# Attention in an interleaved transformer: a wait between two half products moved from VectorE to TensorE, two of four exponentials joined, and a new order of the operations of a key tile

## The chip, the cores and the metric

The kernel runs on one core of one Trainium2 chip. The metric is the device time of one execution in microseconds. Before the change three runs gave a median of 3538.99 us (3538.1 to 3539.18).

## The reference

Two layers are computed, each an attention block and a squared-ReLU block, on 2048 rows of 640 numbers, with 32 heads of 20 numbers. In short:

```python
def A(x, wqkv, wo):                       # 32 heads, Dh = 20
    q, k, v = split_heads(x @ wqkv)
    scores = einsum("bhqd,bhkd->bhqk", q, k) * Dh ** -0.5
    o = einsum("bhqk,bhkd->bhqd", softmax(scores), v)
    return merge_heads(o) @ wo

def B(x, w1, b1, w2, b2):
    h = maximum(x @ w1 + b1, 0)
    return (h * h) @ w2 + b2

for _ in range(2):
    x = x + A(layernorm(x))
    x = x + B(layernorm(x))
```

## The kernel before, in words

The work of a layer comes in stages: the products that give q, k and v; attention; the output product; the squared-ReLU block. The change touches attention alone.

**Blocks and tiles.** Heads are taken four at a time (8 groups) and queries 512 at a time (4 blocks of queries), so a layer has 32 blocks (`NBLK`). A block passes over the 2048 keys in 16 key tiles of 128 keys. The four heads of a group are h = 2p + par: `par` says in which half of TensorE's rows the head's q and k stand (rows 0 to 63 or 64 to 127), and `p` which of two tiles of numbers there. Two matmuls with different `par` use different rows of the array and can run at once.

**What one key tile needs.** Four score products (`score`, 128 keys x 512 queries, one for each head), each followed by an exponential on ScalarE from PSUM to SBUF; then the product with v (`pv`: four heads in four column groups of the array, eight matmul records in the profile since these run in full fp32). The row of ones beside v gives the sum of the exponentials.

**The maxima.** The softmax subtracts a maximum over the keys for each query. It is found two blocks ahead: further products of queries and keys (`by_queries`, the queries now in the partitions), which VectorE reduces to their maxima. Most are done a pair at a time: `smax` makes one 128 x 512 product and one reduction for each `par`. When a layer is in its steady part, 12 such pairs fall on 8 key tiles: 8 pairs as whole products (operations "m" for par 0 and "n" for par 1), and 4 pairs in halves. An operation "u" makes a 128 x 256 product of par 0 in the left half of a PSUM bank, an operation "w" the matching one of par 1 in the right half of the same bank, and one reduction takes both (`smax_half`). Since matmuls on two halves of the array's rows must not write to one bank at once, "w" waits for "u". Before the change this wait went through VectorE: a `nop` in VectorE's queue waits for the matmul of "u", and the matmul of "w" waits for that `nop`.

**What sets the order.** The order of issue is written out by hand as a string in `ORDERS`, one letter an operation: "a" and "b" are the next score products of par 0 and par 1, "m", "n", "u", "w" are those above, "V" is the product with v, which is one key tile behind the scores. In the steady part one string, that for 12 pairs, is repeated for 992 of the 1024 key tiles of the two layers (the last block of each layer uses `both_heads`, which has exponentials of two banks at once already). Each engine works its own queue in the order of issue; an instruction that waits holds those behind it.

**PSUM.** Eight banks: before the change the scores go round banks 0 to 3 (`ps_st`), so a score product waits for the exponential four before it. The products for the maxima use banks 4 to 6 (`turn`), and bank 7 holds the sum of "V". At the end of a block ScalarE copies bank 7 to SBUF (`finish`), and the first "V" of the next block waits for that copy.

In the profile of before, line 481 is `by_queries`, 596 the score product, 603 its exponential, 608 the product with v, 493 and 521 the reductions of whole products and of halves, 517 the `nop`, 621 the copy of bank 7, 1158 and 1165 the wide version in the last block of a layer.

Of the kernel before, what the change touches and what calls it, by code (L numbers as in the profile page):

```python
# [10 lines left out]
AF = mybir.ActivationFunctionType  # L11
# [21 lines left out]
SCALE = DH ** -0.5  # L33
# [6 lines left out]
def tile_layers(  # L40
# [11 lines left out]
    nc = tc.nc  # L52
# [42 lines left out]

    ps_st = Ring(0, 1, 2, 3)
    ps_pj = Ring(4, 5, 6, 7)
# [398 lines left out]

    halved = {}

    def two_columns(t):
# [11 lines left out]
    def smax_half(bank, t, p, sub, c, half, par, earlier=None):  # L511
# [9 lines left out]
        nc.vector.tensor_reduce(  # L521
            maxima(t)[:, p : p + 3 : 2, sub, c if not half else column(t, p, sub)],
            bank.rearrange("q (r k) -> q r k", r=2),
            axis=AX.X,
            op=ALU.max,
        )

    def step_one(t, p, sub, x, par):
# [55 lines left out]

    free = []

    def score(t, kt, h, es):

        p, par = divmod(h, 2)
        if p not in es:  # L590
            es[p] = weights[len(e_n) % len(weights)]
            e_n.append(t)
        dst = banks[:, free.pop(0), :] if free else ps_st("st")
        b = 64 * par
# [7 lines left out]
        )  # L602
        nc.scalar.activation(es[p][:, par, :], dst, AF.Exp, scale=SCALE)  # L603

    def pv(acc, t, kt, es, heads=(3, 2, 1, 0)):
        for h in heads:
            p, par = divmod(h, 2)
            nc.tensor.matmul(  # L608
                acc[32 * h : 32 * h + 32, :],
                v_t[t // NQB, kt // 8][:, kt % 8, 32 * h : 32 * h + 32],  # L610
                es[p][:, par, :],
                start=(kt == 0),
                stop=(kt == NKT - 1),
            )
# [100 lines left out]
    def qkv(first, x_src, rest, scores):  # L715
# [277 lines left out]
        13: "baanmbVmbanambbnbmVanbmnaVnaabnmbVanbmaanVnmbbanaVmnbmabVabbmmnaVm",  # L993
        12: "mbubanawV" * 8,
    }

    def attention(first, x_src, first_rows):
# [146 lines left out]
        def both_heads(p):  # L1144
# [6 lines left out]
            es = es_of.setdefault(i, {})  # L1151
            es[p] = weights[len(e_n) % len(weights)]
            e_n.append(t)
            state["bank"] = (state["bank"] + 2) % 6
            dst = banks[:, state["bank"] : state["bank"] + 2, :]
            for par in range(2):
# [7 lines left out]
                )  # L1164
            nc.scalar.activation(es[p], dst, AF.Exp, scale=SCALE)  # L1165
            if p:
# [13 lines left out]

        free.extend((5, 6))
        for o in "abab":
# [377 lines left out]
```

## Time and profile before

| | |
|---|---|
| median of three runs | 3538.99 us |
| the profiled execution's own time | 3538.19 us |
| its span in the trace | 3536.2 us |
| granted TensorE clock | 1.00 in every stretch |
| busy: TensorE matmul, VectorE, ScalarE, GpSimd | 3521.2, 2731.2, 2652.9, 809.5 us |
| the two steady stretches of attention (first to last 128 x 512 exponential) | 309.9 to 1340.4 us, 2066.2 to 3097.4 us |
| in the stretch 500 to 1000 us: TensorE, VectorE, ScalarE busy | 500.0, 460.1, 498.5 of 500 us |

Times in the trace are microseconds from the start of the span. TensorE's matmuls are pipelined, so their records overlap and its busy share says little; the starts of its matmuls tell its pace. A record of an instruction on ScalarE or VectorE may begin before the one ahead of it has ended, so their pace is read from the ends.

### The profile page before, as it was taken

How to read it: one execution, taken by the hardware profiler on the slowest of the kernel's cores; microseconds unless marked ns; L12 is line 12 of the kernel's file. 1: busy time of each engine (PE TensorE's matmuls, PEld its weight loads, DVE VectorE, ACT ScalarE, POOL GpSimd, SP SyncE). 2: the span in 40 equal slices, each digit the busy share in tenths (PEclk: the TensorE clock that was granted, in tenths of full speed). 3: DMA queues.
4: the chain of work that ended last, by engine and by line, in shares of the span. 5: the costliest groups of instructions: out<-in, count | busy, mean ns of one | idle time of the engine just before them, and what ended most of it. 6: DMA issues, size and time to landing. Idle time of an engine off the chain costs nothing.

```text
span 3536.2 us, 70757 instructions
## 1 busy us (share of the span) xinstructions
PE 3521.2 (100%) x26542; PEld 2264.2 (64%) x26542; DVE 2731.2 (77%) x5023; ACT 2652.9 (75%) x5208; POOL 809.5 (23%) x927
## 2 busy tenths in 40 slices
PE   9999999999999999999999999999999999999999
PEld 7897444444444446999988964444444444479998
DVE  8878999999999993456567789999999999824443
ACT  3778999999999995122237789999999999932221
POOL 6531444221221111111153201221211211211110
PEclk9999999999999999999999999999999999999999
DMA  9776555323211136734477652232232111376231
GB/s 304 274 233 175 172 156 157 109 70 82 57 48 49 46 110 209 249 106 111 135 269 249 197 150 76 65 82 61 67 82 59 46 48 43 115 226 238 75 82 38
DMA packets 377413, 452.78 MB, mean 128 GB/s; under 512 B 176642, under 2 KB 223746, under 8 KB 377070
## 3 DMA queue, kind: packets, MB, share of 16 engines
q1 hardware_dynamic: 376254, 445.89, 41.6%
q8 instruction: 209, 3.42, 0.4%
q10 hardware_dynamic: 816, 2.36, 0.2%
q14 instruction: 134, 1.10, 0.1%
HBM read 273.83 MB, written 174.30 MB: 127 GB/s over the span
## 4 chain that ended last, share of the span: by engine, by line
PE 95%; DVE 2%; ACT 1%; DMA 1%; issue 1%; POOL 0%; SPq 0%; DVEq 0%; ACTq 0%
PE banks L608 29%; PE banks L481 22%; PE banks L293 13%; PE banks L596 11%; PE banks L1326 10%; PE banks L331 9%; DVE mx L493 1%; ACT e L603 1%; PE banks L1158 0%; DMA q<-d_qk 0%; ACT e L1165 0%; DVE bst L244 0%; DVE xnT L257 0%; DVE x L252 0%; DMA d_qk<-ev 0%
## 5 line engine op out<-in xcount | busy, mean ns | idle before, releaser
L603 ACT ACTIVATE e<-banks 128x512 f32<-128x512 f32 x3968 | 2034.7, 613 | 10.3 <-PE banks L596 2.2
L493 DVE TENSOR_REDUCE mx<-banks 128x1 f32<-128x512 f32 x2094 | 1346.5, 686 | 187.2 <-PE banks L596 126.6
L481 PE MATMUL banks<-k,q 60*128 60x512 f32 x4568 | 1347.7, 374 | 3.0 <-DVE v L377 1.7
L481 PEld LDWEIGHTS banks<-k,q 60*128 60x128 f32 x4568 | 763.8, 184 | 848.5 <-DVE mx L493 824.8
L596 PE MATMUL banks<-q,k 62*128 62x512 f32 x3968 | 1132.1, 432 | 0.4 <-DVE mx L541 0.4
L608 PE MATMUL banks<-e,vg 128*32 128x512 f32 x8192 | 1091.0, 605 | 1.5 <-ACT e L1165 1.5
L596 PEld LDWEIGHTS banks<-q,k 62*128 62x128 f32 x3968 | 654.5, 184 | 99.8 <-ACT e L603 36.6
L521 DVE TENSOR_REDUCE mx<-banks 128x2 f32<-128x512 f32 x982 | 670.5, 683 | 0.0
L541 DVE CUSTOM_DVE_ANT_0 rl<-banks,rl 128x512 f32<-128x512 f32 x510 | 332.8, 689 | 101.1 <-PE banks L481 91.0
L1311 ACT ACTIVATE r<-banks,b_t 128x512 f32<-128x512 f32 x96 | 66.2, 689 | 420.1 <-PE banks L293 396.3
L331 PE MATMUL banks<-xnT,wqk 64*128 64x512 f32 x2400 | 378.8, 394 | 0.3 <-ACT mark_t L333 0.3
L533 ACT ACTIVATE rl<-banks 128x512 f32<-128x512 f32 x510 | 270.8, 597 | 98.2 <-PE banks L481 89.3
L1326 PE MATMUL banks<-w,h 128*128 128x320 f32 x2304 | 340.4, 309 | 0.0
L1326 PEld LDWEIGHTS banks<-w,h 128*128 128x128 f32 x2304 | 339.2, 188 | 1.2
L293 PE MATMUL banks<-xnT,w 128*128 128x512 f32 x1440 | 329.4, 389 | 0.0
L331 PEld LDWEIGHTS banks<-xnT,wqk 64*128 64x128 f32 x2400 | 286.1, 185 | 34.2 <-issue 2.4
L293 PEld LDWEIGHTS banks<-xnT,w 128*128 128x128 f32 x1440 | 269.6, 188 | 55.3
L608 PEld LDWEIGHTS banks<-e,vg 128*32 128x32 f32 x8192 | 161.1, 108 | 165.5 <-issue 78.4
L652 POOL TENSOR_TENSOR few<-few,minus_t 128x16 f32<-128x16 f32 x62 | 179.8, 2900 | 357.9 <-DMA few<-d_s 352.5
L271 POOL CAST mr<-nt 128x32 fp32r<-128x32 f32 x64 | 13.4, 209 | 963.7 <-DVE nt L567 963.7
L331 PE MATMUL banks<-wv,xnT 64*128 64x320 f32 x1920 | 199.4, 307 | 0.9 <-ACT mark_t L333 0.9
L331 PEld LDWEIGHTS banks<-wv,xnT 64*128 64x128 f32 x1920 | 187.3, 185 | 2.5 <-ACT mark_t L333 1.4
(89 smaller groups left out, 2094.2 us busy)
## 6 DMA issues: line engine op xcount, KB each, us to landing
q<-d_qk SPq DMA_DIRECT2D x242, 240.0 KB
d_qk<-ev SPq DMA_DIRECT2D x80, 512.0 KB
k<-d_qk SPq DMA_DIRECT2D x152, 240.0 KB
x<-d_x SPq DMA_DIRECT2D x84, 320.0 KB
d_qk<-ev SPq DMA_DIRECT2D x80, 256.0 KB
d_o<-ot SPq DMA_DIRECT2D x248, 80.0 KB
ot<-d_o SPq DMA_DIRECT2D x38, 512.0 KB
d_v<-v SPq DMA_DIRECT2D x32, 512.0 KB
```

The lines of the kernel that those rows point to most:

```text
L293: nc.tensor.matmul(dst, a, b, start=(n == 0), stop=(n == last))
L331: m = nc.tensor.matmul(ch["dst"][:, :width], *pair, start=first, stop=last)
L481: return nc.tensor.matmul(dst, q_t[t][b : b + 60, p, sub * P : (sub + 1) * P], k_t[t // NQB, c][b : b + 60, p, keys], start=True, stop=True,)
L493: nc.vector.tensor_reduce(maxima(t)[:, 2 * par + p, sub, c : c + 1], dst, axis=AX.X, op=ALU.max)
L521: nc.vector.tensor_reduce(maxima(t)[:, p : p + 3 : 2, sub, c if not half else column(t, p, sub)], bank.rearrange("q (r k) -> q r k", r=2), ...
L533: nc.scalar.activation(res, dst, AF.Relu)
L541: nc.vector.tensor_tensor_reduce(out=r, in0=dst, in1=r, scale=1.0, scalar=LEAST, op0=ALU.add, op1=ALU.max, accum_out=maxima(t)[:, 2 * par ...
L596: nc.tensor.matmul(dst, k_t[t // NQB, kt // 4][b : b + 62, p, (kt % 4) * P : (kt % 4 + 1) * P], q_t[t][b : b + 62, p, :], start=True, stop ...
L603: nc.scalar.activation(es[p][:, par, :], dst, AF.Exp, scale=SCALE)
L608: nc.tensor.matmul(acc[32 * h : 32 * h + 32, :], v_t[t // NQB, kt // 8][:, kt % 8, 32 * h : 32 * h + 32], es[p][:, par, :], start=(kt == 0 ...
L652: nc.gpsimd.tensor_tensor(few, few, minus_t, op=ALU.pow)
L1326: nc.tensor.matmul(dst[:, :HALF], hs[f][:, hx, i * P : (i + 1) * P], w_2.piece(at_2(f0 + f, hw, hf)), start=(f == 0 and (hx, hw) == THREE[0]),
```

## The change

Three things change, all in attention.

- The wait of "w" for "u". The matmul of "u" now adds one to a semaphore of its own, `first_half`, and the matmul of "w" waits on TensorE itself for its count. The `nop` on VectorE is gone.
- The exponentials. Each score product now has a bank of its own (`SPOT`): head 1 bank 0, head 3 bank 1, head 0 bank 2, head 2 bank 3. Heads 1 and 2 keep an exponential of 128 x 512 each; heads 3 and 0, which are issued second and third and stand in the neighbouring banks 1 and 2, get one of 128 x 1024. The number of banks for scores, four, is the same. The buffers of exponentials are paired in another way (`es`), with the same number of them.
- The order of a key tile goes from "mbubanawV" to "bumbawnaV".

```diff
-    ps_st = Ring(0, 1, 2, 3)
...
+    first_half = tc.alloc_semaphore("first_half")
+    firsts_done = [0]
...
         if earlier is None:
-            mark = nc.vector.nop()
-            after(mark, m)
-            return mark
-        after(m, earlier, "matmuls on two halves of the rows write to one bank in turn")
-        nc.vector.tensor_reduce(
+            firsts_done[0] += 1
+            m.then_inc(first_half, 1)
+            tc.no_tile_sem_insts.add(m.ins.name)
+            tc.add_to_no_dep_group(f"first half {firsts_done[0]}", m.ins)
+            return m, firsts_done[0]
+        m_1, n = earlier
+        m.wait_op(first_half, n, "sem-ge")
+        tc.declare_no_dep(m.ins, m_1.ins, reason="waits for the semaphore of the first half")
+        tc.declare_fence(m.ins, group=f"first half {n}")
+        r = nc.vector.tensor_reduce(
...
+    SPOT = {(0, 1): 0, (1, 1): 1, (0, 0): 2, (1, 0): 3}
 
     def score(t, kt, h, es):
 
         p, par = divmod(h, 2)
-        if p not in es:
-            es[p] = weights[len(e_n) % len(weights)]
+        pair = "two" if p == par else "one"
+        if pair not in es:
+            es[pair] = weights[len(e_n) % len(weights)]
             e_n.append(t)
-        dst = banks[:, free.pop(0), :] if free else ps_st("st")
+        alone = bool(free) or pair == "one"
+        es[h] = es[pair][:, 1 - par if p == par else p, :]
+        dst = banks[:, free.pop(0) if free else SPOT[p, par], :]
...
-        nc.scalar.activation(es[p][:, par, :], dst, AF.Exp, scale=SCALE)
+        if alone:
+            nc.scalar.activation(es[h], dst, AF.Exp, scale=SCALE)
+        elif 3 - h in es:
+            nc.scalar.activation(es[pair], banks[:, 1:3, :], AF.Exp, scale=SCALE)
...
-        12: "mbubanawV" * 8,
+        12: "bumbawnaV" * 8,
...
-        free.extend((5, 6))
+        free.extend((5, 6, 0, 1))
```

How the rows move is seen in one key tile of TensorE's queue. In these rows 128x512 at line 481 (480 after the change) is "m" or "n", 128x256 is "u" or "w", line 596 (607) is a score product, line 608 (621) the product with v, of which four make one "V". In brackets is what an instruction waits for, by the name of the counter: `Activation_49` counts ScalarE's instructions, `DVE_49` VectorE's, `DVE_sequencer_49` the `nop`. TensorE before:

```order
L481 MATMUL banks<-k_4785,q_9896 128x512 [waits DVE_49]
L596 MATMUL banks<-q_9390,k_5479 128x512 [waits Activation_49]
L481 MATMUL banks<-k_4785,q_9896 128x256 [waits DVE_49]
L596 MATMUL banks<-q_9390,k_5479 128x512 [waits Activation_49] x2
L481 MATMUL banks<-k_4785,q_9896 128x512 [waits DVE_49]
L596 MATMUL banks<-q_9390,k_5479 128x512 [waits Activation_49]
L481 MATMUL banks<-k_4785,q_9896 128x256 [waits DVE_sequencer_49]
L608 MATMUL banks<-e_4746,vg_9233 32x512 x2
L608 MATMUL banks<-e_4745,vg_9233 32x512 x2
```

and now:

```order
L607 MATMUL banks<-q_8345,k_5236 128x512 [waits Activation_49]
L480 MATMUL banks<-k_4472,q_8595 128x256 [waits DVE_49]
L480 MATMUL banks<-k_4472,q_8595 128x512 [waits DVE_49]
L607 MATMUL banks<-q_8345,k_5236 128x512 [waits Activation_49]
L607 MATMUL banks<-q_8345,k_5236 128x512
L480 MATMUL banks<-k_4472,q_8595 128x256 [waits first_half]
L480 MATMUL banks<-k_4472,q_8595 128x512 [waits DVE_49]
L607 MATMUL banks<-q_8345,k_5236 128x512 [waits Activation_49]
L621 MATMUL banks<-e_4746,vg_8698 32x512
L621 MATMUL banks<-e_4745,vg_8698 32x512 x2
L621 MATMUL banks<-e_4746,vg_8698 32x512
```

The half product "u" now comes second in the tile, straight behind the "V" of the tile ahead and one score product. "w" stands three places behind it, as before four, and is no longer the last ahead of "V". The third score product has no wait of its own any more, since the second's covers both banks.

On ScalarE two key tiles before are eight exponentials, here with the copy of bank 7 ahead of them:

```order
L621 COPY o_8658<-banks 128x512 [waits DMAHW6_49,DMAHW1_49,DMAHW7_49,DMAHW0_49,PE_49]
L603 ACTIVATE e_4747<-banks 128x512 [waits PE_49]
L603 ACTIVATE e_4748<-banks 128x512 [waits PE_49]
L603 ACTIVATE e_4747<-banks 128x512 [waits PE_49]
L603 ACTIVATE e_4748<-banks 128x512 [waits PE_49]
L603 ACTIVATE e_4743<-banks 128x512 [waits PE_49]
```

and now six:

```order
L634 COPY o_9333<-banks 128x512 [waits DMAHW5_49,PE_49,Pool_49]
L615 ACTIVATE e_4747<-banks 128x512 [waits PE_49]
L617 ACTIVATE e_4748<-banks 128x1024 [waits PE_49,Activation_49]
L615 ACTIVATE e_4747<-banks 128x512 [waits PE_49]
L615 ACTIVATE e_4743<-banks 128x512 [waits PE_49]
L617 ACTIVATE e_4744<-banks 128x1024 [waits PE_49,Activation_49]
L615 ACTIVATE e_4743<-banks 128x512 [waits PE_49]
```

One instruction a key tile is gone. The wide one waits for TensorE and for an exponential of ScalarE's own: that is the wide one of three key tiles earlier, which wrote to the same buffer.

More of the change, by code (lines that the diff above doesn't have):

```diff
@@ L526, in smax_half @@
         )
+        tc.declare_no_dep(r.ins, m_1.ins, reason="waits for the second half, which waits for the first")
     def step_one(t, p, sub, x, par):
@@ L602, in score @@
         )
-        nc.scalar.activation(es[p][:, par, :], dst, AF.Exp, scale=SCALE)
+        if alone:
+            nc.scalar.activation(es[h], dst, AF.Exp, scale=SCALE)
+        elif 3 - h in es:
+            nc.scalar.activation(es[pair], banks[:, 1:3, :], AF.Exp, scale=SCALE)
     def pv(acc, t, kt, es, heads=(3, 2, 1, 0)):
         for h in heads:
-            p, par = divmod(h, 2)
             nc.tensor.matmul(
@@ L610, in pv @@
                 v_t[t // NQB, kt // 8][:, kt % 8, 32 * h : 32 * h + 32],
-                es[p][:, par, :],
+                es[h],
                 start=(kt == 0),
@@ L1151, in both_heads @@
             es = es_of.setdefault(i, {})
-            es[p] = weights[len(e_n) % len(weights)]
+            e = weights[len(e_n) % len(weights)]
             e_n.append(t)
+            es[2 * p], es[2 * p + 1] = e[:, 0, :], e[:, 1, :]
             state["bank"] = (state["bank"] + 2) % 6
@@ L1164, in both_heads @@
                 )
-            nc.scalar.activation(es[p], dst, AF.Exp, scale=SCALE)
+            nc.scalar.activation(e, dst, AF.Exp, scale=SCALE)
             if p:
```

## The prediction

> **What bounds the kernel now.** I read the page first (span, busy times, chain), then the groups of instructions by line in the middle of attention, then the timeline of one key tile engine by engine, and last the starts of "V" over a block's end.
>
> ```profile
> span 3536.2 us, 70757 instructions
> PE 3521.2 (100%) x26542; PEld 2264.2 (64%) x26542; DVE 2731.2 (77%) x5023; ACT 2652.9 (75%) x5208; POOL 809.5 (23%) x927
> PE 95%; DVE 2%; ACT 1%; DMA 1%; issue 1%; POOL 0%; SPq 0%; DVEq 0%; ACTq 0%
> L603 ACT ACTIVATE e<-banks 128x512 f32<-128x512 f32 x3968 | 2034.7, 613 | 10.3 <-PE banks L596 2.2
> L493 DVE TENSOR_REDUCE mx<-banks 128x1 f32<-128x512 f32 x2094 | 1346.5, 686 | 187.2 <-PE banks L596 126.6
> ```
>
> The page alone would mislead. It gives TensorE 100% and 95% of the chain, yet by its group row ScalarE sits idle for only 10.3 us ahead of 3968 exponentials. Four of those make a key tile, so the changed string covers 992 tiles. The lines of one layer tell their pace (count, shortest, median and longest duration, first and last start):
>
> ```profile
> L603 ACT ACTIVATE e<-banks x1984: 589/603/732, 309.9 to 1340.4; 128x512 f32<-128x512 f32 x199
> ```
>
> 1030.5 us for 496 tiles is 2.077 us a tile. Which engine sets that? First TensorE, one tile (start, length):
>
> ```profile
> 801.80 0.49 PE L481 MATMUL banks<-k,q 60*128 60x512 f32 x1
> 801.80 0.49 PE L596 MATMUL banks<-q,k 62*128 62x512 f32 x1
> 802.13 0.28 PE L481 MATMUL banks<-k,q 60*128 60x256 f32 x1
> 802.13 0.51 PE L596 MATMUL banks<-q,k 62*128 62x512 f32 x2
> 802.37 0.39 PE L481 MATMUL banks<-k,q 60*128 60x512 f32 x1
> 802.48 0.43 PE L596 MATMUL banks<-q,k 62*128 62x512 f32 x1
> 802.60 0.31 PE L481 MATMUL banks<-k,q 60*128 60x256 f32 x1
> 802.85 1.06 PE L608 MATMUL banks<-e,vg 128*32 128x512 f32 x8
> 803.84 0.49 PE L481 MATMUL banks<-k,q 60*128 60x512 f32 x1
> ```
>
> Two rows of work run side by side, par 0 and par 1; scores and maxima take 1.05 us (801.80 to 802.85), "V" 0.99 (to 803.84). In each half of the rows the first product takes 0.33 before the next starts, later whole ones 0.24 (802.13 to 802.37): the first has 0.10 of weight load uncovered (0.49 long against 0.39).
>
> Now ScalarE. Windows around single exponentials give pairs, whose ends I use (start, length of two):
>
> ```profile
> 801.27 1.10 ACT L603 ACTIVATE e<-banks 128x512 f32<-128x512 f32 x2
> 801.75 1.21 ACT L603 ACTIVATE e<-banks 128x512 f32<-128x512 f32 x2
> 802.36 1.09 ACT L603 ACTIVATE e<-banks 128x512 f32<-128x512 f32 x2
> 802.86 1.08 ACT L603 ACTIVATE e<-banks 128x512 f32<-128x512 f32 x2
> 803.33 1.09 ACT L603 ACTIVATE e<-banks 128x512 f32<-128x512 f32 x2
> 803.81 1.20 ACT L603 ACTIVATE e<-banks 128x512 f32<-128x512 f32 x2
> ```
>
> The ends are 802.37, 802.96, 803.45, 803.94, 804.42, 805.01: steps of 0.49, and one of 0.59 a tile. So ScalarE could do four in 1.96 and waits 0.10 for the tile's first score, which ends at 801.80 + 0.49. That wait is too short to be seen as idle. Neither engine alone is the bound. Two loads of weights show how they hold each other:
>
> ```profile
> 802.42 0.18 PEld L596 LDWEIGHTS banks<-q,k 62*128 62x128 f32 x1
> 802.52 0.18 PEld L481 LDWEIGHTS banks<-k,q 60*128 60x128 f32 x1
> ```
>
> The load for the tile's last score product starts 0.05 after the fourth exponential of the tile before has left the bank (802.37). From there "V" is 0.43 away, and 0.99 later the next tile begins. This closes a ring over two tiles: from a tile's start to the end of its first exponential 1.16 (801.80 to 802.96), three more at 0.49 to 804.42, 0.05, 0.43, 0.99: 4.09 for two tiles, 2.045 each. The starts of "V" show it:
>
> ```profile
> 842.26 1.06 PE L608 MATMUL banks<-e,vg 128*32 128x512 f32 x8
> 844.36 1.07 PE L608 MATMUL banks<-e,vg 128*32 128x512 f32 x8
> 846.76 1.06 PE L608 MATMUL banks<-e,vg 128*32 128x512 f32 x8
> 848.80 1.06 PE L608 MATMUL banks<-e,vg 128*32 128x512 f32 x8
> 850.87 1.07 PE L608 MATMUL banks<-e,vg 128*32 128x512 f32 x8
> 852.90 1.07 PE L608 MATMUL banks<-e,vg 128*32 128x512 f32 x8
> ...
> 857.01 1.07 PE L608 MATMUL banks<-e,vg 128*32 128x512 f32 x8
> ```
>
> Tiles of 2.04, 2.07 and 2.03 alternate, 2.0525 on average (848.80 to 857.01, four tiles). The short ones, 2.03, are TensorE's own pace; the long ones wait for ScalarE. Twice a block a tile takes more, 2.10 and 2.40 (842.26 to 846.76), since ScalarE must fit in the copy of bank 7:
>
> ```profile
> 843.69 0.62 ACT L621 COPY o<-banks 128x512 f32<-128x512 f32 x1
> ```
>
> 14 tiles at 2.0525 and two in 4.50 make 33.24 us a block, 2.077 a tile: the whole stretch is accounted for.
>
> **The change part by part.** *The exponentials.* A tile's four become two of 128x512 and one of 128x1024. Wide ones run already in the last block of each layer, with the same extra wait for an older exponential:
>
> ```profile
> L1165 ACT ACTIVATE e<-banks x64: 1018/1212/1405, 1341.1 to 3126.5; 128x1024 f32<-128x1024 f32 x64
> 1343.41 27.64 ACT L1165 ACTIVATE e<-banks 128x1024 f32<-128x1024 f32 x30
> ```
>
> Thirty in a row end 27.64 after the first began; less 1.02 for the first (the shortest), 29 steps of 0.918. Two narrow ones cost 0.98, so joining saves 0.06 a tile on ScalarE. In the ring one tile's last three exponentials are now 0.92 + 0.49 in place of 3 x 0.49: 1.16 + 0.92 + 0.49 + 0.05 + 0.43 + 0.99 = 4.04 for two tiles, 2.02 each. That is below TensorE's 2.03, so ScalarE's hold on the ordinary tiles should end, and with 14 of 16 tiles that is where the gain lies. Weighed against a page: The Trainium skill (ScalarE: Activation LUTs, What ACT_TABLE_LOAD costs) gives an activation with immediate scale and bias 186 ns fixed, of which back-to-back ones overlap about 93, so one fewer would save an estimated 93 ns where the rows here say 60; by it the sum below would be 3510 in place of 3512.
>
> *Banks.* Head 1's bank is read by the exponential ahead of the wide one, so its next product finds it free early. The products of heads 3 and 0 wait for the wide one, which ends 1.16 + 0.92 = 2.08 after its tile's start; with 0.05 that is 0.10 into the next tile at a pace of 2.03. Head 3's load would go out about there anyway (its product's turn is at 0.33, and a load needs 0.10): up to 0.13 of lateness is covered. Cost nothing; without this cover each ns would delay both products.
>
> *The order.* The halves of the rows stay equally loaded. Par 0 has "u", "m", "a", "a", par 1 "b", "b", "w", "n": 256 and three times 512 columns on either side, as before. No product, load or reduction is added, so TensorE's own pace stays 2.03; I allow 2.02 to 2.03 and take 2.027. No DMA and no instruction of another queue moves past one it waits for.
>
> *The wait.* The nop costs VectorE nothing that ends late (it is the sequencer's, and VectorE had slack, below). What matters is how soon "w" can follow "u". Before, "u" ended at 802.41 (802.13 + 0.28) and the load for "w" began at 802.52: 0.11 by way of two hops, through VectorE. Now it is one hop, but "u" is first in its half: done at 0.28 + 0.10 = 0.38 after the tile's start. The turn of "w" comes behind two scores at 0.33 + 0.24 = 0.57, so its load must begin by 0.47: a margin of 0.09. Held up behind a late "w" are "n", the last score and "V", so lateness goes straight into the tile. No row shows TensorE waiting for itself. Below, a hop cannot be less than nothing, and the one from ScalarE to a load is 0.05: on time, cost nothing. Above, two hops in 0.11: "w" 0.02 late, a tile of 2.05, and the gain is gone. I take 0.05, since that row is one hop to the same queue.
>
> A page speaks against that choice. The Trainium skill (Perfetto Trace Analysis, Tensor Engine Instruction) says that a matmul's recorded end is computed, and that its semaphore goes out only when PSUM has acknowledged the last bytes; the 0.38 above may then be too early, and no run here shows by how much.
>
> *VectorE.* Its reductions of one tile, and the next:
>
> ```profile
> 802.33 1.29 DVE L493 TENSOR_REDUCE mx<-banks 128x1 f32<-128x512 f32 x2 [0.17 <-PE banks L596]
> 803.53 0.68 DVE L521 TENSOR_REDUCE mx<-banks 128x2 f32<-128x512 f32 x1
> ```
>
> Starts 0.60 apart, 0.69 for a first one: 1.89 in a tile, with 0.17 idle before. "m" now follows "u", so its reduction begins 0.12 later, at 0.65; the third ends at 0.65 + 1.89 = 2.54. "n" always uses bank 6 now and waits for that: 2.59 with the hop, 0.56 into the next tile, where its turn lets the load begin at 0.57. Just hidden; cost nothing, with no cover left.
>
> *Sum.* Each layer has 31 steady blocks, together 62. Ordinary tiles: 62 x 14 = 868 at 2.0525 - 2.027 = 0.0255 less: 22.1. The two long tiles at a block's end keep the copy, and there ScalarE stays the bound: they lose the 0.06 that the ring loses in two tiles: 62 x 0.06 = 3.7. Together 25.8. The profiled execution took 3538.2 (span 3536.2 and 2 around it), 0.8 under the median of the runs: 3538.2 - 25.8 = **3512 us**.
>
> **Rivals.**
>
> *The wait on TensorE itself is long (slower).* If waiting for its own matmul takes more than the margin, "w" is late in each of 992 tiles. The gain is used up when "w" is about 0.03 late, at a hop of 0.12. If on top of 0.11 the queue has run dry, and the weights of "w" must be loaded uncovered as for a first product (0.10), "w" comes 0.12 late: 2.15 a tile, (2.15 - 2.0525) x 868 - 3.7 = 81 us slower, 3619. For it: "u" ran second in its half before, with three products between it and "w", and is now the first after "V", with less time. Against: two hops took no more than 0.11.
>
> *TensorE sets the pace already (no change).* If the long tiles are long for another reason than ScalarE, or if "w" or "n" comes 0.02 late, ordinary tiles stay at 2.05, and only the block ends gain: 3538.2 - 3.7 = 3534.5. Against: loads that start 0.05 behind an exponential's end, and tiles of 2.03.
>
> *VectorE takes over.* A reduction that ends 0.05 later than worked out would hold "n" by 0.04, a ring over two tiles again: 0.02 a tile. That too is about 2.05 and counts with the case of no change. It could also be that the block's end grows, since extra reductions there meet a VectorE without slack; 0.06 a block would take back the 3.7.
>
> *The change doesn't do what it says.* Were heads 3 and 0 not joined in the steady part, ScalarE would keep 4.09 for two tiles. The rows of the program show one exponential of 128x1024 in every tile, so I give this nothing.
>
> **How the numbers follow.** I give the forecast 0.71, no change (TensorE's or VectorE's pace) 0.14, slower by the wait 0.15. A run of this kernel can be told from no change at about 0.2%, 7 us. Low end: the ring's 2.02 throughout and block ends that gain 0.10: 868 x 0.0325 + 62 x 0.10 = 34, 3504, and a little beyond, 3502. High end: past no change, to "w" late by 0.03 to 0.04: about 3545. The long wait above that, some 0.1, and a tenth below or so are left out.
>
> **What would show it.** Right: starts of "V" 2.02 to 2.03 apart without the alternation; ScalarE's wait for a tile's first score longer, 0.15 and more; 128x1024 exponentials with starts about 0.9 from the next; the load for "w" within 0.10 of the end of "u". Wrong: the score part over 1.05 long with a hole in par 1 ahead of "w" (the wait), or loads for "n" right behind a reduction's end (VectorE), or tiles that still alternate (ScalarE).

## The result

The change makes the kernel slower: 3584.3 us in the median of four runs (3583.92 to 3586.59) against 3538.55 (3537.24 to 3539.18) for the kernel before. The ratio is 1.0131, with a 95% interval of 1.0114 to 1.0149: 46 us more. The forecast was 3512 us, within 3502 to 3545. The profiled execution took 3586.59 us with a span of 3584.2, 48.0 more than the span before.

The page of the changed kernel, in the rows that answer to those shown of before (span, busy times, chain, the exponentials, the loads of weights for the maxima):

```profile
span 3584.2 us, 69732 instructions
PE 3569.1 (100%) x26544; PEld 2139.5 (60%) x26544; DVE 2721.4 (76%) x5023; ACT 2602.4 (73%) x4218; POOL 808.8 (23%) x927
PE 96%; DVE 1%; DMA 1%; issue 1%; ACT 1%; POOL 0%; SPq 0%; DVEq 0%; POOLq 0%
...
L615 ACT ACTIVATE e<-banks 128x512 f32<-128x512 f32 x1988 | 1195.8, 606 | 107.6 <-issue 1.5
...
L617 ACT ACTIVATE e<-banks 128x1024 f32<-128x1024 f32 x990 | 1011.9, 1022 | 1.2 <-PE banks L607 0.8
L480 PEld LDWEIGHTS banks<-k,q 60*128 60x128 f32 x4570 | 693.9, 184 | 192.5 <-PE banks L480 169.4
```

ScalarE has time to spare. It has 990 instructions fewer, and idles 107.6 us ahead of its narrow exponentials, where 10.3 us stood before. (Most of that is the longer tile: in e1 below, with the same exponentials in a shorter tile, it is 20.9 us.) But a wait stands here that no row of before showed: 169.4 us in which a load of weights for a product of the maxima (line 480) waits for another matmul of the same line. Over the 992 tiles in which "w" waits for "u" that is 0.171 us a tile.

The pace of one layer's tiles, from the wide exponentials (count, shortest, median and longest duration, first and last start):

```profile
L617 ACT ACTIVATE e<-banks x495: 1015/1017/1072, 312.8 to 1363.5; 128x1024 f32<-128x1024 f32 x165
```

1050.7 us for 494 intervals is 2.127 a tile, where before it was 2.077 with the block ends. 0.050 over 992 tiles is 49.6 us, so the whole loss lies in these tiles. The starts of "V" over a block's end:

```profile
853.28 1.06 PE L621 MATMUL banks<-e,vg 128*32 128x512 f32 x8
855.41 1.07 PE L621 MATMUL banks<-e,vg 128*32 128x512 f32 x8
857.53 1.06 PE L621 MATMUL banks<-e,vg 128*32 128x512 f32 x8
859.68 1.07 PE L621 MATMUL banks<-e,vg 128*32 128x512 f32 x8
861.80 1.06 PE L621 MATMUL banks<-e,vg 128*32 128x512 f32 x8
```

The alternation of long and short tiles is gone, and so is the block's end: 2.15 stands there (857.53 to 859.68) among tiles of 2.12 and 2.13. Before, two tiles took 2.10 and 2.40. ScalarE, with time to spare, now takes in the copy of bank 7 nearly unnoticed. So the change costs 0.075 in an ordinary tile (2.127 - 2.0525) and gives 0.23 back at a block's end (4.50 before, 2 x 2.127 + about 0.015 now): 62 x (14 x 0.075 - 0.23) = 51 us against 48.0 measured in the span.

One tile on TensorE, its timeline (start, length):

```profile
801.10 0.49 PE L607 MATMUL banks<-q,k 62*128 62x512 f32 x1
801.10 0.62 PE L480 MATMUL banks<-k,q 60*128 60x256 f32 x2
801.43 0.52 PE L607 MATMUL banks<-q,k 62*128 62x512 f32 x2
801.68 0.38 PE L480 MATMUL banks<-k,q 60*128 60x256 f32 x1
801.80 0.38 PE L607 MATMUL banks<-q,k 62*128 62x512 f32 x1
801.90 0.39 PE L480 MATMUL banks<-k,q 60*128 60x512 f32 x1
802.23 1.06 PE L621 MATMUL banks<-e,vg 128*32 128x512 f32 x8
803.22 0.49 PE L607 MATMUL banks<-q,k 62*128 62x512 f32 x1
803.23 0.38 PE L480 MATMUL banks<-k,q 60*128 60x256 f32 x1
```

The first row is the first score product ("b", par 1). The second holds "u" and, behind it in the same half, "m". The 256-column row at 801.68 is "w". The last two rows begin the next tile, where "u" is seen by itself. The score part takes 1.13 (801.10 to 802.23), where 1.05 was the measure before; "V" still takes its 0.99. "w" is the late one, and its load says why:

```profile
801.68 0.18 PEld L480 LDWEIGHTS banks<-k,q 60*128 60x128 f32 x1 [0.17 <-PE banks L480]
```

It begins 0.585 into the tile (from unrounded times; the rows give 801.68 - 801.10). The prediction's limit was 0.47. "u" is 0.38 long, so by the record it ends at 801.48: the load waits 0.20 longer than that. The first score product ends at 801.59, and its exponential goes out 0.04 later:

```profile
801.63 0.60 ACT L615 ACTIVATE e<-banks 128x512 f32<-128x512 f32 x1
```

The load for "w" comes 0.05 behind that. This is where the question for the experiments came from: is a wait of TensorE for its own matmul long (0.20), as the first rival had it, or is the signal of "u" not given before the longer score product, issued 3 ns ahead of it, has ended (0.49)?

### The profile page after: what moved, and what is told of

The parts are those of the page before. It is cut to its first block, busy times and chain, and to the rows that moved or that the text cites. A ratio compares the mean times of both kernels' runs of the same rounds, so it can differ in the third digit from the quotient of the medians.

```text
span 3584.2 us, 69732 instructions
## 1 busy us (share of the span) xinstructions
PE 3569.1 (100%) x26544; PEld 2139.5 (60%) x26544; DVE 2721.4 (76%) x5023; ACT 2602.4 (73%) x4218; POOL 808.8 (23%) x927
## 4 chain that ended last, share of the span: by engine, by line
PE 96%; DVE 1%; DMA 1%; issue 1%; ACT 1%; POOL 0%; SPq 0%; DVEq 0%; POOLq 0%
PE banks L621 28%; PE banks L607 19%; PE banks L480 17%; PE banks L292 13%; PE banks L330 9%; PE banks L1340 9%; DMA q<-d_qk 0%; PE banks L1172 0%; ACT e L1179 0%; DVE bst L243 0%; DVE mx L492 0%; DVE xnT L256 0%; DVE x L251 0%; DMA d_qk<-ev 0%; SPq L76 0%
## 5 line engine op out<-in xcount | busy, mean ns | idle before, releaser
L492 DVE TENSOR_REDUCE mx<-banks 128x1 f32<-128x512 f32 x2092 | 1425.2, 685 | 243.4 <-PE banks L480 237.5
L480 PE MATMUL banks<-k,q 60*128 60x256 f32 (+1 forms) x4570 | 1418.7, 390 | 1.8 <-DVE mx L474 1.2
L615 ACT ACTIVATE e<-banks 128x512 f32<-128x512 f32 x1988 | 1195.8, 606 | 107.6 <-issue 1.5
L607 PE MATMUL banks<-q,k 62*128 62x512 f32 x3968 | 1087.0, 420 | 1.2 <-DVE mx L548 0.7
L607 PEld LDWEIGHTS banks<-q,k 62*128 62x128 f32 x3968 | 588.7, 184 | 832.1 <-ACT e L617 770.6
L617 ACT ACTIVATE e<-banks 128x1024 f32<-128x1024 f32 x990 | 1011.9, 1022 | 1.2 <-PE banks L607 0.8
L480 PEld LDWEIGHTS banks<-k,q 60*128 60x128 f32 x4570 | 693.9, 184 | 192.5 <-PE banks L480 169.4
```

The source lines that it names most:

```text
L480: return nc.tensor.matmul(dst, q_t[t][b : b + 60, p, sub * P : (sub + 1) * P], k_t[t // NQB, c][b : b + 60, p, keys], start=True, stop=True,)
L492: nc.vector.tensor_reduce(maxima(t)[:, 2 * par + p, sub, c : c + 1], dst, axis=AX.X, op=ALU.max)
L607: nc.tensor.matmul(dst, k_t[t // NQB, kt // 4][b : b + 62, p, (kt % 4) * P : (kt % 4 + 1) * P], q_t[t][b : b + 62, p, :], start=True, stop ...
L615: nc.scalar.activation(es[h], dst, AF.Exp, scale=SCALE)
L617: nc.scalar.activation(es[pair], banks[:, 1:3, :], AF.Exp, scale=SCALE)
```

## The experiments

Two theories went into the runs. **Theory A**: TensorE gives its signals in the order of issue, across the two halves of its rows. "u" (256 columns) runs beside the score product (512 columns) issued just ahead, and signals only after that one. Put "u" ahead of the score product and the signal comes at 0.38. **Theory B**, the first rival of the prediction: a wait of TensorE for TensorE is slow in itself, because the signal comes late or the queue runs dry, and any order with so short a way from "u" to "w" pays for it.

The results together. The time of the load for "w" and the length of an ordinary tile are in us, the load from the tile's start; two lengths mean that tiles alternate; the ratio is to the kernel before, on the same chip.

| run | order of a tile | "w" waits by | exponentials | load of "w" | tile | median us | ratio and 95% interval |
|---|---|---|---|---|---|---|---|
| before | mbubanawV | nop | four | 0.725 | 2.03, 2.07 | 3538.55 | 1 |
| after | bumbawnaV | TensorE | three | 0.585 | 2.127 | 3584.30 | 1.0131 (1.0114 to 1.0149) |
| e1 | ubmbawnaV | TensorE | three | 0.437 | 2.016 | 3498.73 | 0.9887 (0.9872 to 0.9901) |
| e2 | mbubanawV | TensorE | three | 0.67 | 2.01, 2.035 | 3507.61 | 0.9910 (0.9895 to 0.9925) |
| e3 | mbubanawV | TensorE | four | 0.67 | 2.01, 2.10 | 3537.77 | 0.9995 (0.9985 to 1.0005) |
| e4 | mbubanawV | nop | three | 0.725 | 2.036 | 3520.24 | 0.9947 (0.9933 to 0.9962) |
| e5 | bumbanawV | TensorE | three | on time | 2.02, 2.12 | 3540.06 | 1.0008 (0.9999 to 1.0018) |
| e6 | bumbawnaV | nop | three | 0.64 | 2.183 | 3646.57 | 1.0309 (1.0293 to 1.0324) |
| e7 | bumbawnaV | nop | four | 0.64 | 2.183 | 3645.76 | 1.0305 (1.0287 to 1.0322) |
| e8 | ubmbanawV | TensorE | three | on time | 2.01, 2.12 | 3539.07 | 1.0004 (0.9994 to 1.0013) |
| e9 | ubmbawnaV | TensorE | four | on time | 2.02, 2.055 | 3523.56 | 0.9955 (0.9940 to 0.9970) |
| e10 | ubmbawnaV | nop | three | 0.50 | 2.040 | 3526.05 | 0.9961 (0.9946 to 0.9976) |
| e11 | bucmbawnaV | TensorE | three | 0.447 | 2.015, 2.06 | 3522.46 | 0.9950 (0.9934 to 0.9967) |
| e12 | bcumbawnaV | TensorE | three | 0.592 | 2.133 | 3596.56 | 1.0161 (1.0146 to 1.0176) |

### e1: "u" one place earlier

The changed kernel with its first two operations swapped.

```diff
-        12: "bumbawnaV" * 8,
+        12: "ubmbawnaV" * 8,
```

> The change with one letter moved: the first half product "u" is issued ahead of the first score product instead of behind it ("ubmbawnaV"). Theory A (signals come in the order of issue): in the changed kernel the signal of "u", whose recorded end is 0.38 us after the tile's start, was held until the 512-column score product issued 3 ns before it had ended at 0.49, and came 0.09 after that. With "u" first it is free at 0.38, the load for "w" begins about 0.47, a tile takes 2.03 to 2.05 instead of 2.127, and the kernel 3515 to 3530 us. Theory B (a wait of TensorE for its own matmul costs 0.20 whatever stands ahead): the load stays at 0.58, the tile at 2.127, the time at 3584.

Measured: 3498.73 us (3497.69 to 3500.93), 40 us under the kernel before and 86 under the change. A swap of two neighbours that start in the same instant turns a loss of 46 us into the fastest kernel of this study. One tile on TensorE, then the loads (the row of 0.33 is two loads):

```profile
800.68 0.38 PE L480 MATMUL banks<-k,q 60*128 60x256 f32 x1
800.68 0.49 PE L607 MATMUL banks<-q,k 62*128 62x512 f32 x1
...
801.25 0.28 PE L480 MATMUL banks<-k,q 60*128 60x256 f32 x1
```

```profile
801.11 0.33 PEld L480 LDWEIGHTS banks<-k,q 60*128 60x128 f32 x2
```

"u" ends at 801.06 by the record; the load for "w" begins at 801.11, 0.05 later and within the limit of 0.47, and "w" itself then runs in its turn at 0.57. So a wait of TensorE for its own matmul costs 0.05 to 0.06, about what the prediction took from the hop from ScalarE. Theory B falls, theory A stands. The time is 16 us below the expected range: the load was expected 0.09 behind the end of "u", as it stood behind the score product in the change, and came after 0.06 (why is told under "One line through all runs").

### e2, e3, e4, e7: one part of the change at a time

The change is made of three parts. e2 is the changed kernel with the old order, e3 the kernel before with the new wait alone, e4 the kernel before with the joined exponentials alone, e7 the kernel before with the new order alone.

```diff
# e2, from the change
-        12: "bumbawnaV" * 8,
+        12: "mbubanawV" * 8,
# e3, from the kernel before
-            mark = nc.vector.nop()
-            after(mark, m)
-            return mark
-        after(m, earlier, "matmuls on two halves of the rows write to one bank in turn")
+            firsts_done[0] += 1
+            m.then_inc(first_half, 1)
...
+        m_1, n = earlier
+        m.wait_op(first_half, n, "sem-ge")
# e4, from the change: the old order, and the nop back in place of the semaphore
-            m.then_inc(first_half, 1)
...
+            mark = nc.vector.nop()
+            after(mark, m)
...
-        12: "bumbawnaV" * 8,
+        12: "mbubanawV" * 8,
# e7, from the kernel before
-        12: "mbubanawV" * 8,
+        12: "bumbawnaV" * 8,
```

> The change with the old order of a key tile ("mbubanawV"); joined exponentials and the wait on TensorE stay. "u" then starts at 0.33 of the tile and ends at 0.61, behind products that end at 0.49, and the turn of "w" comes at 0.80, its load 0.10 earlier. Theory A: the load for "w" 0.09 behind the end of "u", at 0.70, just on time: a tile of 2.03 to 2.04, 3510 to 3520 us, faster than before. Theory B: the load 0.20 behind, at 0.81, "w" 0.11 late and "V" with it: 2.13 a tile, about 3585.

> The kernel before with the wait on TensorE's own semaphore alone (four narrow exponentials, old order). Theory A: the load for "w" comes 0.09 behind the end of "u" instead of 0.11, which is under or at the ring's pace: 3530 to 3539 us, no change. Theory B: 0.20 behind, "w" about 0.1 late: 2.13 to 2.15 a tile, 3585 to 3605.

> The kernel before with the joined exponential alone (the nop on VectorE and the old order stay). It has no wait of TensorE for itself, so theories A and B agree. If the ring over ScalarE set the long tiles, as the prediction had it, they fall to 2.03: about 3512 us. If TensorE's own pace set them, only the block ends gain: 3535.

> The kernel before with the new order alone (nop on VectorE and four narrow exponentials stay). Theory A: the nop sees "u" at 0.53, the load for "w" comes at 0.60, 2.13 to 2.15 a tile: 3585 to 3605 us, so that the order alone holds the whole loss. Otherwise (signal at 0.42): the ring over ScalarE as before, 2.05 to 2.08 a tile, 3530 to 3545 us.

Measured: 3507.61, 3537.77, 3520.24 and 3645.76 us. The joined exponentials alone gain 18 us, the new wait alone nothing, both together 30. The new order alone loses 108. e3 came as expected; e2 is 2 us below its range, e4 lies between its two expected times, 8 us above the nearer, and e7 is taken up with e6. Two readings of these traces matter. First the starts of "V" with the new wait alone (e3):

```profile
848.63 1.07 PE L616 MATMUL banks<-e,vg 128*32 128x512 f32 x8
850.73 1.06 PE L616 MATMUL banks<-e,vg 128*32 128x512 f32 x8
852.74 1.06 PE L616 MATMUL banks<-e,vg 128*32 128x512 f32 x8
854.84 1.06 PE L616 MATMUL banks<-e,vg 128*32 128x512 f32 x8
```

The short tiles are 2.01 now, no longer 2.03, and the long ones 2.10 in place of 2.07. Their sum is the same 4.10, as a ring over two tiles by way of ScalarE demands: what one tile gains the next one waits. This shows that 2.03 was not TensorE's own pace. In the kernel before, the `nop` held "w" even in the short tiles (load at 0.725, where the turn of "w" as last product wants it at about 0.70); with the semaphore it comes at 0.67. Then the joined exponentials alone (e4):

```profile
848.54 1.07 PE L613 MATMUL banks<-e,vg 128*32 128x512 f32 x8
850.58 1.07 PE L613 MATMUL banks<-e,vg 128*32 128x512 f32 x8
852.61 1.07 PE L613 MATMUL banks<-e,vg 128*32 128x512 f32 x8
854.66 1.06 PE L613 MATMUL banks<-e,vg 128*32 128x512 f32 x8
```

The alternation is gone: ScalarE's ring no longer binds, and all tiles are 2.03 to 2.05, which is the `nop`. So each of the two parts takes away one of two limits that lie 0.02 apart, and only both together reach 2.022 on average (e2). There the tiles alternate once more, 2.01 and 2.035; the sum, 4.045, is close to the 4.04 that the prediction worked out for the ring with joined exponentials. The 3507.61 of e2 is near the 3512 that the prediction had counted on for the whole change. The 77 us between e2 and the change are the order's.

### e6: the nop in the new order

The changed kernel with the `nop` through VectorE in place of the semaphore, as in the diff of e4, order unchanged.

> The change with the old wait by a nop on VectorE (joined exponentials and new order stay). The nop's record tells when the signal of "u" is seen by another engine. Theory A: at 0.53 of the tile, 0.04 behind the end of the first score product (0.49), and the load for "w" 0.07 later at 0.60, 0.02 later than in the change: 2.13 to 2.15 a tile, 3585 to 3605 us. If only a wait of TensorE for its own product is late, the nop is seen at 0.42, 0.04 behind the recorded end of "u" at 0.38, the load comes at 0.49, and the tile is 2.03 to 2.05: 3510 to 3530 us.

Measured: 3646.57 us, which misses the expected range on the upper side by about 40; e7 misses it likewise. The tile on TensorE and the load for "w":

```profile
802.74 0.49 PE L599 MATMUL banks<-q,k 62*128 62x512 f32 x1
```

```profile
803.38 0.18 PEld L480 LDWEIGHTS banks<-k,q 60*128 60x128 f32 x1 [0.23 <-DVEq L516]
```

The load is at 0.64 in place of 0.585. Here it is VectorE's sequencer that waits for "u", not TensorE, and it too is not released before the score product has ended (802.74 + 0.49 = 803.23; the `nop` runs 0.57 into the tile). So the lateness belongs to the signal of "u" and not to the kind of waiter, which is a second and independent blow to theory B. With two hops behind the signal "w" is simply later than with one. The miss was in the size: I had taken 0.04 from the score's end to the `nop`, as for ScalarE, and it was about 0.08. That e6 and e7 have the same time and the same tile, 2.183, says more: with "w" this late, joining the exponentials gains nothing (3646.57 against 3645.76). The ring over ScalarE, 2.045 a tile with four, is shorter than such a tile.

### e5 and e8: "w" last again

The prediction's margin for the load would be wider if "w" stood behind "n" and the last score product, as before. e5 does that to the change, e8 to e1.

```diff
# e5
-        12: "bumbawnaV" * 8,
+        12: "bumbanawV" * 8,
# e8
-        12: "bumbawnaV" * 8,
+        12: "ubmbanawV" * 8,
```

> The change with "w" moved behind "n" and the last score product ("bumbanawV"); "u" stays second, behind the first score. Theory A (the signal of "u" is held until the score product issued ahead of it has ended, 0.49 into the tile): "w" can be loaded from about 0.58 on as in the change, but its turn is now at 0.80, its load 0.10 earlier, so nothing is late: 2.02 to 2.03 a tile, 3500 to 3512 us. If a wait of TensorE for itself stalled the queue whatever its length, the tile would stay near 2.127 and the time near 3584.

> "u" ahead of the first score and "w" last ("ubmbanawV"), with joined exponentials and the wait on TensorE. With "u" first the load for "w" came 0.06 behind its end and was no longer late, so more room for "w" should bring nothing: 3496 to 3503 us, the same as "u" first alone (3498.7). If "w" still cost something there, this one is faster by 0.01 to 0.02 a tile: 3480 to 3490 us.

Measured: 3540.06 and 3539.07 us, both no different from the kernel before and both outside what I had expected. "w" is on time in both, and of the 46 us that the change lost e5 wins back all but 2; but a new limit appears. In e8 the starts of "V", then VectorE's reduction of the halves, the load for "n", and the products "u" (the tile's start) and "n":

```profile
848.68 1.06 PE L621 MATMUL banks<-e,vg 128*32 128x512 f32 x8
850.81 1.06 PE L621 MATMUL banks<-e,vg 128*32 128x512 f32 x8
852.81 1.06 PE L621 MATMUL banks<-e,vg 128*32 128x512 f32 x8
```

```profile
799.65 0.68 DVE L527 TENSOR_REDUCE mx<-banks 128x2 f32<-128x512 f32 x1
```

```profile
800.38 0.18 PEld L480 LDWEIGHTS banks<-k,q 60*128 60x128 f32 x1 [0.16 <-DVE mx L527]
```

```profile
799.81 0.38 PE L480 MATMUL banks<-k,q 60*128 60x256 f32 x1
...
800.39 0.49 PE L480 MATMUL banks<-k,q 60*128 60x512 f32 x1
```

With "w" last, the reduction of the halves is last on VectorE, and it ends at 800.33, 0.52 into the next tile. The load for "n" follows it by 0.05, at 0.57. But "n" is now third in its half, where its turn is 0.57 and its load is wanted by 0.47: it comes 0.10 late, and its weights are uncovered (0.49 long in place of 0.39). Every second tile is 2.11 to 2.13, in turn with tiles of 2.00 to 2.02. In e5 the same load stands behind the same reduction (801.49 + 0.68 = 802.17, load at 802.22). This is the prediction's rival "VectorE takes over", in the very place that it named, the wait of "n" for a reduction. It was not part of the change, where "w" stands ahead of "n"; it becomes true when the order is mended in the wrong way.

### e9 and e10: the best order with one part taken back

e9 is the kernel before with the new wait and the order of e1 (four exponentials); e10 is e1 with the `nop`.

```diff
# e9, from the kernel before, beside the semaphore as in e3
-        12: "mbubanawV" * 8,
+        12: "ubmbawnaV" * 8,
# e10, from the change, beside the nop as in e6
-        12: "bumbawnaV" * 8,
+        12: "ubmbawnaV" * 8,
```

> "u" first and the wait on TensorE, but four narrow exponentials as before: what the joined exponential is worth in the good order. The ring over ScalarE is back at 4.09 for two tiles while nothing else is late: tiles alternate around 2.045 to 2.05, the block ends cost 4.50 as before: 3525 to 3540 us, so that joining is worth 30 to 40 us of the 40 gained. If TensorE's order alone made the gain, this comes near 3500.

> "u" first and joined exponentials, but the wait by a nop on VectorE. In the runs so far a tile lasts 1.54 us longer than the time at which the load for "w" begins, once that is later than 0.47 (0.585 gives 2.127, 0.64 gives 2.183). The nop's two hops take 0.11 instead of 0.06, so the load begins at about 0.49: 2.03 to 2.04 a tile, some 0.02 over "u" first with the wait on TensorE: 3510 to 3520 us. If the route of the signal doesn't matter, 3499.

Measured: 3523.56 and 3526.05 us. e9 against e1 prices the joined exponentials once more: 24.8 us, less than the 30 to 40 expected, and e9 is 1 us below its range. The alternation is back in e9 (2.02 and 2.055), as the ring with four exponentials has it. e10 prices the semaphore in this order: 27 us, since with the `nop` the load for "w" comes at 0.50, just past the limit of 0.47, and the tile is 2.040. The time is 6 us beyond the expected 3510 to 3520: the tile came at the upper end of what was worked out, 0.024 over e1 and not 0.02, and the two tiles at a block's end take about 4.46 where e1 has about 4.40.

### e11 and e12: the score product cut in two

The strongest form of theory A: if it is the end of the score product ahead that holds the signal of "u", then a shorter product ahead must let it go earlier, with "u" where the change has it. In both kernels the first score product is made as two matmuls of 256 columns, one after the other in the same bank. In e11 "u" is issued between the two (behind 256 columns), in e12 behind both (512 columns, as in the change). The diff is e11's; e12 differs in the order alone, "bcumbawnaV", where "c" is the second half of the score product. The same numbers are computed, with one matmul and one load of weights more in each tile.

```diff
-    def score(t, kt, h, es):
+    def score(t, kt, h, es, cut=None):
...
+        cols = cut or slice(0, QB)
...
-            dst,
+            dst[:, cols],
...
-            q_t[t][b : b + 62, p, :],
+            q_t[t][b : b + 62, p, cols],
...
+        if cut and not cut.start:
+            return
...
-        12: "bumbawnaV" * 8,
+        12: "bucmbawnaV" * 8,
...
-                score(i // NKT, i % NKT, 2 * p + par, es_of.setdefault(i, {}))
+                args = (i // NKT, i % NKT, 2 * p + par, es_of.setdefault(i, {}))
+                if o == "b" and not p and not free:
+                    score(*args, slice(0, QB // 2))
+                    rest.append(args)
+                else:
+                    score(*args)
+            elif o == "c":
+                if rest:
+                    score(*rest.pop(), slice(QB // 2, QB))
```

> The change with the first score product made as two of 256 columns, "u" issued between them; the same results, one matmul and one weight load more a tile. Theory A (the signal of "u" waits for the end of the matmuls issued ahead): what stands ahead is now as short as "u" and ends with it at 0.38, so the load for "w" begins at 0.44 to 0.48 though "u" is still behind a score: 2.02 to 2.04 a tile, 3500 to 3520 us. If being second, behind a score, were what delays it: 2.127 and 3584.

> The same with both halves of the first score ahead of "u". The same instructions, one place changed. Theory A: the second half ends at about 0.50, the signal of "u" comes behind it, the load for "w" at 0.58 to 0.60: 2.12 to 2.15 a tile, 3580 to 3610 us. If the splitting itself made the difference, this one is as fast as the one with "u" between.

Measured: 3522.46 and 3596.56 us, e11 2 us above its range and e12 within its own. e11, the two halves of the score product (line 608), "u" at 801.87, and the load for "w":

```profile
801.87 0.38 PE L608 MATMUL banks<-q,k 62*128 62x256 f32 x1
801.87 0.38 PE L480 MATMUL banks<-k,q 60*128 60x256 f32 x1
802.09 0.28 PE L608 MATMUL banks<-q,k 62*128 62x256 f32 x1
```

```profile
802.31 0.18 PEld L480 LDWEIGHTS banks<-k,q 60*128 60x128 f32 x1
```

and e12:

```profile
801.13 0.38 PE L608 MATMUL banks<-q,k 62*128 62x256 f32 x1
801.13 0.38 PE L480 MATMUL banks<-k,q 60*128 60x256 f32 x1
801.35 0.28 PE L608 MATMUL banks<-q,k 62*128 62x256 f32 x1
```

```profile
801.72 0.18 PEld L480 LDWEIGHTS banks<-k,q 60*128 60x128 f32 x1 [0.17 <-PE banks L480]
```

The matmul rows are the same three in both; only their order of issue differs, and the records do not show it. The load for "w" does: 0.447 into the tile in e11, 0.06 behind the end of the first half (802.25), and 0.592 in e12, 0.09 behind the end of the second (801.63). In e11 "u" is second in the tile, as in the change, so it is not its place behind a product as such that delays it. e12 taken alone could also be read in another way: that "u" really starts later, behind the start of the second half, though its record begins at 801.13. In the change no product starts between the tile's start and "u", so that reading doesn't explain the change itself. And "m", which runs behind "u" in the same half of the rows, is not later: its reduction begins 0.657 into the tile in e12 and 0.658 in the change, against 0.654 in e1. So "u" is computed when its record says, and only its signal is late.

e11 stands 24 us above e1 although "w" is on time. Its tiles alternate, 2.015 and 2.06. The extra load and the second half's later end may delay the first exponential. Which wait is the last one there is not shown and stays open.

### One line through all runs

In the runs where "w" stands ahead of "n" and the tiles do not alternate (e9 and e11 do), the tile's length follows the load for "w":

| run | e1 | e10 | after | e12 | e6, e7 |
|---|---|---|---|---|---|
| load of "w" | 0.437 | 0.50 | 0.585 | 0.592 | 0.64 |
| tile | 2.016 | 2.040 | 2.127 | 2.133 | 2.183 |
| tile less load | 1.579 | 1.540 | 1.542 | 1.541 | 1.543 |

Wherever it is late the tile is the load's time plus 1.54; where it is on time the tile is 2.016 (e1). The two meet at 2.016 - 1.542 = 0.474. That is the prediction's limit of 0.47, found there from two rows. Whether TensorE or ScalarE's ring, 2.02 by the prediction, sets the 2.016 of e1 the runs do not tell.

The traces also keep the moment at which each semaphore is counted up, which the views above do not print. This is the signal itself, and it settles what the loads only suggest (medians over the tiles from 700 to 1100 us, from the tile's start):

| run | count for the matmul issued ahead of "u" | count for "u" | behind the recorded end of "u" | load of "w" behind the count |
|---|---|---|---|---|
| e1 | none ahead | 0.397 | 0.014 | 0.043 |
| e11 | no count on the half ahead | 0.405 | 0.019 | 0.043 |
| after | 0.508 | 0.542 | 0.157 | 0.043 |
| e12 | 0.514 | 0.548 | 0.159 | 0.042 |

The load follows the count by 0.04 in all four, so the hop is always the same. With no product ahead that ends later, the count comes 0.014 to 0.019 behind the recorded end of "u". With such a product ahead it comes 0.034 behind the count for that product. This explains the 0.06 from end to load in e1 and the 0.09 in the change, and also why the `nop` of e6 came 0.08 and not 0.04 behind the end of the score product.

## Why the prediction was wrong

**The step that failed is "The wait".** The prediction took "u" to be "done at 0.28 + 0.10 = 0.38 after the tile's start", added 0.05 for the hop, found that the load must begin by 0.47, a margin of 0.09, and wrote "on time, cost nothing". The limit was right (0.474) and the hop was right (0.05 to 0.06, e1 and e11). The 0.38 was not: the score product ahead ended at 0.49, its count came at 0.508 and that for "u" only at 0.542, so the load began at 0.585. The margin of 0.09 was used up and the load came 0.11 beyond the limit, in each of 992 tiles. In the prediction's own sum the term "ordinary tiles", 22.1 us of gain, becomes 868 x (2.127 - 2.0525) = 65 us of loss, of which the block's ends give 14 back.

The Trainium skill (TensorE: Matmul & The Clock Gate, Part 3, The mechanism) states that matmuls keep the order of the program in their starts and in their ends. That is the rule that spoke against the change and that I did not weigh. The records of this trace don't agree with it on their face, since "u" ends at 801.48 and the score product ahead of it at 801.59; the counts do, and so do the waits, with 0.585 in the change against 0.437 in e1, and 0.592 in e12 against 0.447 in e11. That holds for the ends; by the recorded starts the last score product, issued behind "n", stands ahead of it (801.80 against 801.90). The page of the Trainium skill that the prediction did name (Perfetto Trace Analysis, Tensor Engine Instruction), by which a recorded end is computed, was a warning at the right place for another reason. With nothing longer ahead the signal comes only 0.014 behind the recorded end (e1, and e2 and e3 with the old order); it was the order of the signals that made it 0.157 in the change, and with the hop 0.20 to the load.

**The rival came in its place, but only in part by its mechanism.** "The wait on TensorE itself is long" priced a tile of 2.15 and 3619 us. The tile came at 2.127. One part of it came true: the weights of "w" are loaded uncovered (its row is 0.38 long in the change and 0.28 in e1). What was to make "w" late, a slow wait of the engine for itself, is refuted by e1 (0.05) and by e6 (VectorE as the waiter sees it late too). Against the profiled execution its time was 33 us too high: 868 x 0.023 = 20 of that is the tile, and 10 that it gave the block's ends only 3.7 us, where a late "w" leaves ScalarE so much time that they gain 62 x 0.23 = 14.

**The exponentials were right in the main.** Predicted: 25.8 us for the sum that rests on them. Measured: 18 with the `nop` (e4), 25 in the order of e1 (e9 to e1), 30 with the semaphore in the old order (e3 to e2), and nothing where "w" is late (e7 to e6). The ring's 2.02 stands in e2 as 2.022. ScalarE's hold on the ordinary tiles ended in the change and in e4, where the tiles no longer alternate; in e2 a faint alternation is left, at the ring's pace.

**"TensorE's own pace stays 2.03" was wrong, by 0.02 and in the change's favour.** The short tiles of the kernel before were held by the `nop`; TensorE can do 2.01 (the short tiles of e3). With it goes the sentence that the `nop` "costs VectorE nothing that ends late": true of VectorE, but TensorE waited for it. It costs nothing where ScalarE binds anyway (e3), 12.6 us once that is gone (e4 to e2), 27 in the order of e1 (e10 to e1) and 62 in the order of the change (e6 to the change).

**That the order adds nothing was wrong** only through the wait: the same eight products, but "u" behind a longer one and "w" sooner. e1 has the same set of products in nearly the same order, and its tile is 2.016.

**The rest.** The reduction of "m" was to begin at 0.65 and did:

```profile
801.75 0.69 DVE L492 TENSOR_REDUCE mx<-banks 128x1 f32<-128x512 f32 x1 [0.24 <-PE banks L480]
```

(801.10 + 0.65.) The rival "VectorE takes over" did not come true in the change; it did in e5 and e8. The banks cost nothing that could be seen in e1 and e2. Of the signs that the prediction named for being wrong, the one that it put first appeared: a score part over 1.05 with a hole in par 1 ahead of "w".

The best version is e1: the whole change, with "u" issued one place earlier, 3498.73 us, 1.1% under the kernel before.

## What to carry to other kernels

When one matmul's signal is waited for within a few tenths of a microsecond, as here, count the time to the end of every longer matmul issued ahead of it, also of one that runs beside it in the other half of the rows, and issue the one that is waited for first. Don't take the recorded end of a matmul as the time of its signal; take the start of what waited for it. Where two limits lie 0.02 us apart, taking away one of them shows little or nothing, so such parts are priced together as well as alone.

## What the runs showed of the hardware

- A 256-column matmul issued 3 ns behind a 512-column one on the other half of the rows lets its waiter go 0.585 after the start, and 0.437 when issued ahead of it, though its recorded length is 0.38 in both. With the longer one cut into two of 256 columns it is 0.447 when one of these is ahead, and 0.592 when both are.
- A load of weights that waits for a matmul of TensorE itself begins 0.04 behind that matmul's count on the semaphore. The count comes 0.014 to 0.019 behind the recorded end where no matmul issued ahead ends later (e1, e11), and 0.034 behind the count of that other matmul where one does (after, e12). So the load is 0.06 behind the matmul's own end or 0.09 behind the other's.
